# Attention and a mixture of experts in one kernel: three runs of score units a tile in place of four, and the values in one piece

## Chip, cores and metric

The kernel runs on one core of a Trainium2 chip. The metric is the device time of one execution in microseconds (us). The engines are named as in the profile: PE (TensorE), DVE (VectorE), ACT (ScalarE), POOL (GpSimd) and SP (SyncE, which here only issues DMAs).

## The reference

Multi-query attention (8 batches, 16 heads, 384 positions, head size 64, one key and value head a batch) is followed by a two-level mixture of experts over the 3072 tokens of 1024 features that come out of it:

```
scores = scale * q @ k.T                 # per batch and head, 384 x 384
attn   = softmax(scores)
x      = (attn @ v), heads side by side  # 3072 x 1024
g      = argmax(x @ w_group)             # one of 4 groups, with its softmax weight g_w
e      = argmax(x @ w_expert[g])         # one of 4 experts of the group, weight e_w
out    = g_w * e_w * (relu(x @ w1[g, e]) @ w2[g, e])
```

## The kernel before

The attention is worked in *tiles* of 128 query positions for all 16 heads: three tiles a batch, 24 in all (the number `t`). A tile has eight *units* of two heads each (`u`). For a unit, `scores` (L198) makes 128 x 2 x 384 scores in PSUM; `soft` (L212) takes their row maximum on DVE (L217) and their exponentials with row sums on ACT (L220), into a buffer `pr` in SBUF. `norm` (L229) takes the reciprocal of the sums on DVE and multiplies on POOL. `transp` (L239) transposes a unit in 32 x 32 blocks on DVE into `ring`, which holds three half tiles. When all eight units of a tile stand there, `pv` (L246) multiplies them with the values into four PSUM banks, and `pv_out` (L263) copies these to SBUF, and POOL casts them to bf16.

PSUM has eight banks. Before, `ps_s` holds two score buffers of two banks each, and `ps_x` four single banks that `xbank` (L93) hands out in turn for everything else: values, expert matmuls, logits, transposed queries, counts.

All instructions of an engine run in the order in which the program writes them (the scheduler is set to manual). The main loop (L794) goes over *slots*, each of two units, so four slots a tile (`p` is the slot in its tile). In slots 0 and 1 the PE, after the scores, works on the expert of the batch before: `main_expert` is a generator that `advance(n)` (L710) moves on by n groups. A group is one PSUM bank of eight matmuls and its evacuation: 8 groups of the first layer, w1 (L479, 384 columns, relu on ACT in L485), and 6 of the second, w2 (L493, 512 columns, scaled on ACT in L511, here called y groups). In slots 2 and 3 PE does the two halves of the values of the tile before. Other steps hang on a slot and a place in it by `at` and are called by `run`: `logits` and the gate's small operations (`gate_first` on DVE, `gate_choose` on PE, `gate_score` on DVE, ...), which pick the expert that most tokens of the batch need, and the loads of the next q, k, v and of the expert's weights (4 MB, issued by POOL).

Transposed queries come in two ways. For the first five tiles (`TQ = 5`) `q_group` (L174) transposes on PE and copies with ACT (L187); later ones come by a DMA that leaves only a block transpose to DVE, `q_blocks` (L190).

After the last slot, from L827, a tail finishes the last tile, then computes the last batch's main expert, a second expert for the few tokens of it that need one (`few_...`), and a loop for the remaining ones.

Of the kernel before, what the change touches and what calls it, by code (L numbers as in the profile page):

```python
# [19 lines left out]
def kernel(  # L20
# [70 lines left out]
    TQ = 5  # L91

    def xbank():  # L93
        x = ps_x.tile([P, 512], FP32, tag="x", name="x")
        return x

# [100 lines left out]

    def scores(u):  # L198
        b, j, c = units[u]
        qt, kt = st["qt", u // 8, c // 4], st["kt", b]  # L200
        s = ps_s.tile([P, 2, 512], FP32, tag="s")
        cc = c % 4
        for h in range(2):
            r = slice(h * D, (h + 1) * D)
            for m in range(2):
                nc.tensor.matmul(  # L206
                    out=s[m * D:(m + 1) * D, h, 0:S], lhsT=qt[r, ts(2 * cc + m, D)], rhs=kt[r, :],
                    start=True, stop=True, tile_position=(h * D, m * D),
                )
        st["s", u] = s  # L210

    def soft(us, between):  # L212
        ssum = ppool.tile([P, 2, 2], FP32, tag="ssum")
        for k, u in enumerate(us):
            s = st.pop(("s", u))
            nmx = ppool.tile([P, 2], FP32, tag="nmx")
            nc.vector.tensor_reduce(out=nmx[:], in_=s[:, :, 0:S], axis=AX.X, op=ALU.max, negate=True)  # L217
            pr = ppool.tile([P, 2, S], FP32, tag="pr")
            for h in range(2):
                nc.scalar.activation(  # L220
                    out=pr[:, h, :], in_=s[:, h, 0:S], func=ACTF.Exp, bias=nmx[:, h:h + 1], scale=1.0,
                    accum_out=ssum[:, k, h:h + 1],
                )
            st["pr", u] = pr
            if k == 0:
                between()
        st["ssum", us[0]] = ssum

    def norm(us):  # L229
        rinv = ppool.tile([P, 2, 2], FP32, tag="rinv")  # L230
        nc.vector.reciprocal(out=rinv[:], in_=st.pop(("ssum", us[0]))[:])  # L231
# [14 lines left out]
    def pv(t, n0, n1):  # L246
# [3 lines left out]
        if n0 == 0:  # L250
            st["o", t] = [xbank() for _ in range(P // 32)]
        o = st["o", t]
# [10 lines left out]
    def pv_out(t):  # L263
# [6 lines left out]
        for i, o in enumerate(st.pop(("o", t))):  # L270
            nc.scalar.copy(out=xt[:, :, ts(i, 32)], in_=o[:, 0:2 * P].rearrange("p (c q) -> p c q", c=KO))  # L271
        nc.gpsimd.tensor_copy(out=st["xb", b][:, :, ts(j, P)], in_=xt)  # L272
# [254 lines left out]

    def any_bank():
        return bank_end() if st.get("ended") else xbank()[:]

    def main_expert(b, on_act):
# [5 lines left out]

        yield from expert(st["xb", b], w1, w2, scaled(lambda: st["gsel", b][0], store), any_bank, on_act)

# [164 lines left out]

    NSL = NU // 2
    SB = ST * 4
    NT = B * ST
    pending = []

    def advance(groups):  # L710
        for _ in range(3 * groups):
# [19 lines left out]
    for b in range(B):  # L731
        s0 = SB * b
        for x, j0, j1 in ((s0 + 8, 0, 1), (s0 + 16, 1, ST)):
            at(x, "m2", logits, b, j0, j1)
            at(x + 1, "m0" if b and j0 == 0 else "v", logits_out, b, j0, j1)
        at(s0 + 9, "m0" if b else "v", gate_first, b)
        at(s0 + 9, "m3" if b else "m2", gate_choose, b)
        at(s0 + 9, "w", gate_score, b)
        at(s0 + 9, "w", gate_pick, b)
        at(s0 + (13 if b == B - 1 else 12), "w", gate_picked, b)  # L740
        if b == B - 1:
            at(s0 + 9, "w", load_main, b, 0)
            at(s0 + 10, "w", load_main, b, 1)
        else:
            at(s0 + 9, "g", load_main, b, 0)
            at(s0 + 9, "g", load_main, b, 1)
            at(s0 + 16, "g", keep_xb, b)
        at(s0 + 17, "v", gate_masks, b)
        x = s0 + 18
        at(x, "e", gate_values, b)  # L750
        at(s0 + (19 if b == B - 2 else 22), "w", gate_selected, b)
        if b == B - 1:
            at(s0 + 13, "w", gate_pick_second, b)
        if b + 1 < B:
            at(s0 + 2, "g", load_k, b + 1)
            at(s0 + 4, "g", load_v, b + 1)
            at(s0 + 7, "g", scale_k, b + 1)
            at(s0 + 8, "e", k_blocks, b + 1)
    for t in range(NT):
        for x, u, half in ((4 * t, t, 1), (4 * t + 1, t + 1, 0)):  # L760
            if u < TQ:
                at(x, "m1", q_group, u, half)
            elif u < NT:
                at(x, "e", q_blocks, u, half)
        if t < NT - 2:
            at(4 * t, "g", load_q, t + 2)

# [73 lines left out]
    pv(NT - 1, NB // 2, NB)  # L841
    pv_out(NT - 1)
    advance(1)
    load_second(1)
    advance(4)
    run(i + 4, "m2")
    pending.append(main_expert(b, lambda k: k < FO or k % 2 == 0))
    advance(1)
    run(i + 5, "v")
# [6 lines left out]
    advance(2)  # L856
    few_places()
    gate_count()
    advance(1)
    run(i + 6, "e")  # L860
    run(i + 10, "w")
    gate_remaining()
# [26 lines left out]
    )  # L889
    advance(3)  # L890
    few_gather()
    advance(2)
    ls_ps = xbank()
# [68 lines left out]
```

## Time and profile before

| | |
|---|---|
| median of 3 runs | 509.52 us (509.21 to 509.81) |
| the profiled execution, its own time | 508.39 us |
| its span, first to last instruction | 507.0 us |
| mean granted clock of PE | 0.997 of full speed |
| DMA traffic | 84.04 MB, mean 166 GB/s |

An engine's busy time can be read against the span, but PE's matmuls are pipelined and their ends are modelled, so the rows' starts are the safer numbers: the distance from one piece of PE work to the next is what the piece costs. A row of the timeline has its start, its length, engine, line, operation, output and inputs, and in square brackets the idle time of the engine before it and what ended that. In rows of matmuls an fp32 matmul counts twice, since it is issued as two passes.

### The profile page before, as it was taken

What the parts mean: (1) busy time and instruction counts of PE and PEld (TensorE: products, weight loads), DVE (VectorE), ACT (ScalarE), POOL (GpSimd) and SP (SyncE); (2) the same over time, 40 slices, a digit from 0 to 9 for tenths busy, and PEclk for the clock granted to TensorE, in tenths of its full rate; (3) what the DMA queues carried; (4) which work ended last, traced back from release to release, by engine and by line L of the source; (5) the groups of instructions that cost most, each with busy time, mean ns of one, the idle gap of its engine ahead of it and who ended that gap; (6) DMA issues with size and microseconds to landing.
All of it is one profiled execution on the core that took longest, in us unless ns stands there. A gap on an engine that the chain in (4) does not pass through costs nothing.

```text
span 507.0 us, 20054 instructions
## 1 busy us (share of the span) xinstructions
PE 481.5 (95%) x8256; PEld 262.1 (52%) x8273; DVE 413.0 (81%) x737; ACT 321.8 (63%) x1002; POOL 289.6 (57%) x524
## 2 busy tenths in 40 slices
PE   7597789999999999999999999999999999999994
PEld 3143356555456455555465455555455455555653
DVE  3889979988899879988899879998799888890630
ACT  4776766677676766676676776676775775753421
POOL 1665955684576664584576654584476654584300
PEclk9999999999999999999999999999999999999998
DMA  7612997399947998389946998389956993089993
GB/s 106 145 26 45 174 239 193 76 160 233 255 86 129 220 237 218 75 157 232 261 84 123 217 243 223 75 143 230 245 116 111 210 241 110 1 155 241 231 243 121
DMA packets 64524, 84.04 MB, mean 166 GB/s; under 512 B 20379, under 2 KB 39963, under 8 KB 64432
## 3 DMA queue, kind: packets, MB, share of 16 engines
q0 software_dynamic: 19152, 37.84, 41.3%
q1 hardware_dynamic: 44320, 44.61, 35.2%
q8 instruction: 66, 1.08, 0.9%
q10 hardware_dynamic: 960, 0.30, 0.3%
q14 instruction: 26, 0.21, 0.1%
HBM read 101.52 MB, written 19.40 MB: 239 GB/s over the span
## 4 chain that ended last, share of the span: by engine, by line
PE 90%; DVE 5%; ACT 3%; issue 1%; POOL 0%; POOLq 0%; ACTq 0%; DVEq 0%
PE x L257 26%; PE s L206 25%; PE x L479 15%; PE x L493 13%; PE sb L493 4%; PE x L280 3%; ACT pr L220 3%; DVE nmx L217 2%; PE sb L479 2%; DVE ring L241 2%; PE x L674 1%; PE x L100 1%; PE x L689 1%; PE x L145 0%; PE x L643 0%
## 5 line engine op out<-in xcount | busy, mean ns | idle before, releaser
L235 POOL TENSOR_SCALAR pr<-pr,rinv 128x384 f32<-128x384 f32 x384 | 218.3, 588 | 146.0 <-DVE rinv L231 133.2
L220 ACT ACTIVATE pr<-s,nmx 128x384 f32<-128x384 f32 x384 | 218.0, 579 | 131.5 <-DVE nmx L217 120.0
L217 DVE TENSOR_REDUCE nmx<-s 128x2 f32<-128x768 f32 x192 | 174.3, 948 | 45.7 <-PE s L206 44.6
L241 DVE STREAM_TRANSPOSE ring<-pr 128x768 f32<-128x768 f32 x192 | 175.4, 952 | 0.1
L206 PE MATMUL s<-kt,qt 64*64 64x384 f32 x1536 | 148.9, 496 | 13.3 <-ACT pr L220 12.3
L257 PE MATMUL x<-ring,v_sb 32*64 32x256 f32 x4608 | 137.7, 378 | 0.2
L257 PEld LDWEIGHTS x<-ring,v_sb 32*64 32x64 f32 x4608 | 101.6, 131 | 43.0 <-issue 23.2
L206 PEld LDWEIGHTS s<-kt,qt 64*64 64x64 f32 x1536 | 48.5, 132 | 82.6 <-ACT pr L220 44.4
L220 ACT ACTIVATION_READ_ACCUMULATOR pr<-s,nmx 128x1 f32 x384 | 77.9, 203 | 0.0
L479 PE MATMUL x<-xb,w 128*128 128x384 bf16 x448 | 76.6, 326 | 0.0
L479 PEld LDWEIGHTS <-w 128*128 128x128 bf16 x512 | 47.7, 98 | 42.2 <-issue 12.6
L493 PE MATMUL x<-w,h_t 128*128 128x512 bf16 x276 | 64.7, 380 | 0.6
L493 PEld LDWEIGHTS <-h_t 128*128 128x128 bf16 x384 | 35.7, 98 | 52.0 <-issue 11.9
L454 POOL DMA_DIRECT2D w<-in_moe_w_dram x36 | 27.9, 784 | 10.8 <-issue 9.0
L271 ACT COPY xt<-x 128x256 f32<-128x256 f32 x96 | 28.9, 385 | 2.8 <-PE x L257 2.7
L485 ACT ACTIVATE h_t<-x 128x384 bf16<-128x384 f32 x56 | 25.4, 502 | 6.4 <-PE x L479 6.4
L272 POOL CAST xb<-xt 128x1024 bf16<-128x1024 f32 x24 | 24.9, 1036 | 3.6 <-ACT xt L271 3.6
L511 ACT ACTIVATE y<-x,gsel 128x512 f32<-128x512 f32 x36 | 24.8, 693 | 3.1 <-PE x L493 3.1
L195 DVE STREAM_TRANSPOSE qt<-q_sb 128x512 f32<-128x512 f32 x38 | 26.1, 687 | 0.0
L493 PE MATMUL sb<-w,h_t 128*128 128x512 bf16 x92 | 21.2, 379 | 0.2
L231 DVE RECIPROCAL rinv<-ssum 128x4 f32<-128x4 f32 x96 | 13.9, 144 | 3.3 <-ACT pr L220 3.3
L511 ACT ACTIVATE y<-sb,gsel 128x512 f32<-128x512 f32 x9 | 6.2, 688 | 16.1 <-PE sb L493 16.1
(132 smaller groups left out, 165.6 us busy)
## 6 DMA issues: line engine op xcount, KB each, us to landing
w<-in_moe_w_dram POOLq DMA_DIRECT2D x36, 1024.0 KB, 19.6
q_sb<-in_q_dram SPq DMA_DIRECT2D x76, 224.0 KB, 6.0
out_dram<-y SPq DMA_DIRECT2D x96, 128.0 KB, 6.3
xb_scratch<-xb SPq DMA_DIRECT2D x8, 768.0 KB, 4.3
v_sb<-in_v_dram SPq DMA_DIRECT2D x32, 96.0 KB, 4.0
kk<-in_k_dram SPq DMA_DIRECT2D x28, 92.0 KB, 4.1
q_sb<-in_q_dram SPq DMA_DIRECT2D x16, 128.0 KB, 3.3
q_sb<-in_q_dram SPq DMA_DIRECT2D x5, 64.0 KB, 3.1
```

Of the source, the lines that this page charges most:

```text
L195: nc.vector.transpose(out=qt[:].rearrange("p (x d) -> p x d", d=32), in_=q_sb[:, :, 0:32])
L206: nc.tensor.matmul(out=s[m * D:(m + 1) * D, h, 0:S], lhsT=qt[r, ts(2 * cc + m, D)], rhs=kt[r, :], start=True, stop=True, tile_position=(h ...
L217: nc.vector.tensor_reduce(out=nmx[:], in_=s[:, :, 0:S], axis=AX.X, op=ALU.max, negate=True)
L220: nc.scalar.activation(out=pr[:, h, :], in_=s[:, h, 0:S], func=ACTF.Exp, bias=nmx[:, h:h + 1], scale=1.0, accum_out=ssum[:, k, h:h + 1],)
L235: nc.gpsimd.tensor_scalar(out=pr, in0=pr, scalar1=rinv[:, k, h:h + 1], scalar2=1.0, op0=ALU.mult, op1=ALU.mult)
L241: nc.vector.transpose(out=ring[:, (u // 4) % 3, u % 4].rearrange("p h s -> p (h s)"), in_=st.pop(("pr", u))[:].rearrange("p h s -> p (h s)"),)
L257: nc.tensor.matmul(out=o[i][h * D:(h + 1) * D, 0:2 * P].rearrange("d (g c q) -> d g c q", g=2, c=4), lhsT=v_sb[r, n, :], rhs=ring[r, a:z + ...
L271: nc.scalar.copy(out=xt[:, :, ts(i, 32)], in_=o[:, 0:2 * P].rearrange("p (c q) -> p c q", c=KO))
L454: nc.gpsimd.dma_start(out=w[:, o:o + 4, :], in_=(w1f, w2f)[n][ds(e, 1), :, o:o + 4, :].rearrange("o p c f -> (o p) c f"))
L479: nc.tensor.matmul(out=hp[:, 0:S], lhsT=w1[:, ko, ts(fc, P)], rhs=xb[:, ko, :], start=(ko == 0), stop=(ko == KO - 1))
L493: nc.tensor.matmul(out=yp, lhsT=h_t[:, fo, ts(j, P)], rhs=w2[:, fo, ts(nh, 512)], start=(fo == 0), stop=(fo == FO - 1),)
L511: nc.scalar.activation(out=y[:, ts(nh, 512)], in_=yp, func=ACTF.Copy, scale=g)
```

## The change

A tile's eight units now come in three slots, of three, two and three units, in place of four slots of two. The third unit of a slot takes its scores in a buffer `e` of two banks of its own (`ps_e`, through `pair`), and the same buffer serves as two of the four banks of `pv`; `ps_x` shrinks from four banks to two. In slots 0 and 2 of a tile PE works on the expert (six or nine thirds of a group, in three parts, since `advance` now counts thirds), in slot 1 on the values of the tile before, all 12 blocks in one piece. Of a tile's eight transposes three now lie in slot 0 (the last units of the tile before), two in slot 1 and three in slot 2. The fourth of the value copies in `pv_out` goes to DVE (in the tail the second too). The expert of a batch starts at slot 3 of the nine of the next batch, where it was slot 5 of twelve. All hooks move to the new slots; `q_group` of the next tile's first half now lies in the third slot of the tile before, and both `q_blocks` in the middle slot.

```
-    ps_x = ctx.enter_context(tc.psum_pool(name="ps_x", bufs=4))
+    ps_e = ctx.enter_context(tc.psum_pool(name="ps_e", bufs=1))
+    ps_x = ctx.enter_context(tc.psum_pool(name="ps_x", bufs=2))
...
+    def xtile():
+        x = ps_x.tile([P, 512], FP32, tag="x", name="x")
+        return x[:]
+
+    def pair():
+        e = ps_e.tile([P, 2, 512], FP32, tag="e", name="e")
+        return e
+
     def xbank():
-        x = ps_x.tile([P, 512], FP32, tag="x", name="x")
-        return x
+        if not st.get("ended"):
+            return xtile()
+        n = st["banks"] = st.get("banks", -1) + 1
+        if n % 4 == 2:
+            st["pair"] = pair()
+        return st["pair"][:, n % 4 - 2, :] if n % 4 > 1 else xtile()
...
-    def scores(u):
+    def scores(u, spare):
...
-        s = ps_s.tile([P, 2, 512], FP32, tag="s")
+        s = pair() if spare else ps_s.tile([P, 2, 512], FP32, tag="s", name="s")
...
     def soft(us, between):
...
-            if k == 0:
-                between()
+            between(k)
...
         if n0 == 0:
-            st["o", t] = [xbank() for _ in range(P // 32)]
+            e = pair()
+            st["o", t] = [e[:, 0, :], e[:, 1, :], xtile(), xtile()]
...
         for i, o in enumerate(st.pop(("o", t))):
-            nc.scalar.copy(out=xt[:, :, ts(i, 32)], in_=o[:, 0:2 * P].rearrange("p (c q) -> p c q", c=KO))
+            xo, o = xt[:, :, ts(i, 32)], o[:, 0:2 * P].rearrange("p (c q) -> p c q", c=KO)
+            if i == 3 or (st.get("ended") and i == 1):
+                nc.vector.tensor_copy(out=xo, in_=o)
+            else:
+                nc.scalar.copy(out=xo, in_=o)
...
-    NSL = NU // 2
-    SB = ST * 4
+    NSL = B * ST * 3
+    SB = ST * 3
...
+        x = s0 + 6
+        at(x, "v", gate_first, b)
+        at(x, "m2", gate_choose, b)
+        at(x, "w", gate_score, b)
+        at(x, "w", gate_pick, b)
...
     for t in range(NT):
-        for x, u, half in ((4 * t, t, 1), (4 * t + 1, t + 1, 0)):
-            if u < TQ:
-                at(x, "m1", q_group, u, half)
-            elif u < NT:
-                at(x, "e", q_blocks, u, half)
+        if t < TQ:
+            at(3 * t, "m1", q_group, t, 1)
+        if t + 1 < TQ:
+            at(3 * t + 2, "m1", q_group, t + 1, 0)
+        elif t + 1 < NT:
+            at(3 * t + 1, "e", q_blocks, t + 1, 0)
+            at(3 * t + 1, "e", q_blocks, t + 1, 1)
...
+    U0 = (0, 3, 5, 8)
     for i in range(NSL):
-        t, p = i // 4, i % 4
-        if i >= SB + 5 and (i - 5) % SB == 0:
-            pending.append(main_expert((i - 5) // SB - 1, lambda k: True))
-        us = (2 * i, 2 * i + 1)
-        for u in us:
-            scores(u)
+        t, p = i // 3, i % 3
+        if i >= SB + 3 and (i - 3) % SB == 0:
+            pending.append(main_expert((i - 3) // SB - 1, lambda k: True))
+        us = range(8 * t + U0[p], 8 * t + U0[p + 1])
+        ready = [u for u in (range(8 * t - 3, 8 * t), range(8 * t, 8 * t + 2), range(8 * t + 2, 8 * t + 5))[p] if u >= 0]
+        for n, u in enumerate(us):
+            scores(u, n == 2)
         run(i, "s")
-        soft(us, lambda: run(i, "b"))
-        if p < 2:
-            run(i, "m0")
-            advance(1)
-            run(i, "m1")
-            advance(1)
-            run(i, "m3")
-            if p == 1 and t % ST > 0:
-                advance(1)
-        elif t > 0:
-            pv(t - 1, (p - 2) * NB // 2, (p - 1) * NB // 2)
+        if p == 1:
+            soft(us, lambda k: None)
+            if t > 0:
+                pv(t - 1, 0, NB)
+        else:
+            soft(us, lambda k: advance(3) if k == 1 else None)
+            run(i, "m1")
+            advance(2)
+            if ready:
+                transp(ready.pop(0))
+            advance(1)
+            if i % SB in (3, 8):
+                advance(2)
+                if ready:
+                    transp(ready.pop(0))
+                advance(1)
         run(i, "v")
         run(i, "m2")
-        if i >= 2:
-            transp(2 * i - 4)
-            transp(2 * i - 3)
+        for u in ready:
+            transp(u)
         run(i, "w")
         norm(us)
         run(i, "e")
-        if p == 3 and t > 0:
+        if p == 1 and t > 0:
             pv_out(t - 1)
         run(i, "g")
...
     st["ended"] = True
-    transp(2 * i - 4)
-    transp(2 * i - 3)
-    advance(2)
-    transp(2 * i - 2)
-    transp(2 * i - 1)
-    run(i + 1, "w")
-    advance(1)
+    advance(6)
+    for u in range(NU - 3, NU):
+        transp(u)
+    run(i, "w")
     load_second(0)
     few_ready()
     pv(NT - 1, 0, NB // 2)
-    advance(1)
+    advance(3)
     pv(NT - 1, NB // 2, NB)
     pv_out(NT - 1)
-    advance(1)
+    advance(3)
     load_second(1)
```

More of the change, by code (lines that the diff above doesn't have):

```diff
@@ L212, in soft @@
     def soft(us, between):
-        ssum = ppool.tile([P, 2, 2], FP32, tag="ssum")
+        ssum = ppool.tile([P, len(us), 2], FP32, tag=f"ssum{len(us)}", name="ssum", bufs=3)
         for k, u in enumerate(us):
@@ L536, in store @@
                 nc.sync.dma_start(out=out_v[b, j, n], in_=y[32 * n:32 * (n + 1), :])
-        yield from expert(st["xb", b], w1, w2, scaled(lambda: st["gsel", b][0], store), any_bank, on_act)
+        yield from expert(st["xb", b], w1, w2, scaled(lambda: st["gsel", b][0], store), lambda: bank_end() if st.get("ended") else xbank(), on_act)
     def few_ready():
@@ L699, in few_expert, with advance @@
         )
[L705 to L706 removed]
+    NSL = B * ST * 3
+    SB = ST * 3
     NT = B * ST
     pending = []
[L710 to L711 removed]
+    def advance(thirds):
+        for _ in range(thirds):
             while pending:
@@ L732 @@
         s0 = SB * b
-        for x, j0, j1 in ((s0 + 8, 0, 1), (s0 + 16, 1, ST)):
+        last = b == B - 1
+        for x, j0, j1 in ((s0 + 5, 0, 1), (s0 + 11, 1, ST)):
             at(x, "m2", logits, b, j0, j1)
[L735 to L740, printed above, removed]
@@ new lines @@
+        at(s0 + 16, "w", gate_selected, b)
+        if not last:
+            at(s0 + 1, "g", load_k, b + 1)
+            at(s0 + 3, "g", load_v, b + 1)
+            at(s0 + 5, "g", scale_k, b + 1)
+            at(s0 + 7, "e", k_blocks, b + 1)
+    for t in range(NT):
+        if t < TQ:
[5 more added lines that the diff above has]
+            at(3 * t + 1, "e", q_blocks, t + 1, 1)
```

53 lines of the change are left out of this document (23 added, 30 removed).

## The prediction

> **What bounds the kernel now.** I read the page first: the busy line of the engines and the head line of the chain that ended last.
>
> ```profile
> PE 481.5 (95%) x8256; PEld 262.1 (52%) x8273; DVE 413.0 (81%) x737; ACT 321.8 (63%) x1002; POOL 289.6 (57%) x524
> PE 90%; DVE 5%; ACT 3%; issue 1%; POOL 0%; POOLq 0%; ACTq 0%; DVEq 0%
> ```
>
> TensorE carries the chain. A mean hides stages, so next the table by windows: a piece of the head, where no expert work exists yet, and one steady batch of three tiles.
>
> ```profile
> 8.70:23.50 14.80, 8.35 (x74) 2.50 (x72) 11.71 (x18) 11.16 (x37) 8.45 (x15) 1.00 0.69 120
> 190.60:247.80 57.20, 57.10 (x1011) 30.85 (x1011) 50.68 (x86) 38.98 (x123) 35.03 (x61) 1.00 0.84 180
> ```
>
> In the steady batch PE is busy 57.10 of 57.20 us: nothing is gained there by feeding PE sooner, only by giving it less to do. VectorE has 6.5 us to spare. In the head PE works 8.35 of 14.80 us, so a loop over the other engines sets the pace. What PE does in the steady part is in the chain by time (start, us, what):
>
> ```profile
> 247.82 4.01 PE x L479 x24
> 253.28 2.78 PE x L257 x96
> 265.25 1.45 PE s L206 x16
> 266.70 2.71 PE x L479 x16
> 285.65 3.56 PE x L493 x16
> 305.15 4.01 PE x L479 x24
> ```
>
> From 247.82 to 305.15, the same place one batch later, are 57.33 us, without holes. The pieces have a fixed part: w1 matmuls cost (4.01-2.71)/8 = 0.16 each, so 2.71 is 16 x 0.16 + 0.15. A 256-column fp32 pass at that rate (384 columns in 0.16) costs two times 0.107, with eight in the array at once: 96 of them are 12 x 0.213 = 2.56, and the values piece of 2.78 has 0.22 over. Now one slot, from the timeline; this gives every latency that I use.
>
> ```profile
> 252.14 0.15 PEld L206 LDWEIGHTS s<-kt,qt 64*64 64x64 f32 x4 [0.17 <-issue]
> 252.46 0.15 PEld L206 LDWEIGHTS s<-kt,qt 64*64 64x64 f32 x4 [0.17 <-issue]
> 252.82 1.78 DVE L217 TENSOR_REDUCE nmx<-s 128x2 f32<-128x768 f32 x2
> 253.83 0.58 ACT L220 ACTIVATE pr<-s,nmx 128x384 f32<-128x384 f32 x1 [1.33 <-DVE nmx L217]
> 254.53 1.81 DVE L241 STREAM_TRANSPOSE ring<-pr 128x768 f32<-128x768 f32 x2
> 254.96 0.58 ACT L220 ACTIVATE pr<-s,nmx 128x384 f32<-128x384 f32 x1
> 256.27 0.13 DVE L231 RECIPROCAL rinv<-ssum 128x4 f32<-128x4 f32 x1
> 256.50 2.27 POOL L235 TENSOR_SCALAR pr<-pr,rinv 128x384 f32<-128x384 f32 x4 [1.82 <-DVE es L416]
> ```
>
> Half a unit of scores every 0.32, so a unit is 0.64 and a piece of n units 0.17 + 0.64n (two: 1.45). A maximum takes DVE 0.855 (two from 252.82 to 254.53), a transpose 0.87 (two to 256.27), a unit's exponentials 1.13 on ScalarE (253.83 to 254.96), the reciprocal comes 1.31 after the last unit's first exponential, and Pool normalizes a unit in 1.14, beginning 0.23 after it. The head gives the links between engines:
>
> ```profile
> 6.76 1.52 PE L206 MATMUL s<-kt,qt 64*64 64x384 f32 x16 [0.24 <-ACT qt L187]
> 7.71 1.82 DVE L217 TENSOR_REDUCE nmx<-s 128x2 f32<-128x768 f32 x2 [1.51 <-PE s L206]
> 8.70 0.58 ACT L220 ACTIVATE pr<-s,nmx 128x384 f32<-128x384 f32 x1 [1.71 <-DVE nmx L217]
> 9.99 0.88 PE L206 MATMUL s<-kt,qt 64*64 64x384 f32 x8 [1.12 <-ACT pr L220]
> 14.39 0.59 ACT L187 COPY qt<-x 128x512 f32<-128x512 f32 x1
> ```
>
> Scores to maximum 0.95, maximum to exponential 0.99, exponential to a free score buffer 1.29 (1.13 and 0.16 for the signal), and a copy of transposed queries 0.59.
>
> **The change, part by part. (1) Fewer pieces on PE.** A tile goes from four score pieces and two value pieces to three and one: 0.17 + 0.22 = 0.39 us less, 1.17 a batch. Expert pieces stay two a tile. From tile 5 on 19 tiles remain, 6.33 batches: 7.4 us at most.
>
> **(2) New stalls in the steady part.** Rows for what stands near the values:
>
> ```profile
> 250.54 0.88 ACT L485 ACTIVATE h_t<-x 128x384 bf16<-128x384 f32 x2
> 260.34 1.20 ACT L271 COPY xt<-x 128x256 f32<-128x256 f32 x4
> 268.10 0.18 DVE L302 TENSOR_REDUCE mx<-lg 128x5 f32<-128x20 f32 x1
> 268.53 0.18 DVE L306 TENSOR_TENSOR first<-oh 128x16 bf16<-128x16 f32 x1
> 269.24 0.17 PE L341 MATMUL x<-first,ones 128*128 128x16 bf16 x1
> ```
>
> Call T the start of a tile's scores. In its first slot DVE does three maxima from T+0.95 and then three transposes, of the last units of the tile before, to 0.95 + 2.57 + 2.61 = 6.1; all values matmuls wait for them (about T+6.3). PE needs 2.09 for scores, 0.15 + 2.56 for two w1 groups and 1.45 for the next scores: 6.25. With two y groups (3.42) it is 7.1, with three w1 groups 7.5. So DVE just keeps up. The exception is the tile with gate_first: 0.6 us of small operations (268.10 to 268.71) go ahead of two of the transposes, and gate_choose, now on PE behind the groups, waits for them: 5.0 against 4.8, 0.2 lost; then transposes and gate_score end near 6.9 against 6.5, 0.2 more. With only two banks for expert groups the third group of a slot, and logits, wait for the ScalarE evacuation (0.44, row 250.54) behind two units' exponentials: 0.95 + 0.99 + 2.26 + 0.44 + 0.16 = 4.8 against PE's 4.8; I take 0.1 twice. Sum 0.6 a batch; net gain 1.17 - 0.6 = 0.57, over 6.33 batches **-3.6**. The third unit's wait for the two shared banks costs nothing: values end, two copies of 0.30 (1.20 for four) free them by about +1.0, while the other two units' scores hold PE for 1.45. Were ScalarE late, each 0.1 over that would be paid in every tile. The fourth copy moves to DVE: between 0.30 (ScalarE's) and 0.56 (a 384-column PSUM read in the row below); I take 0.35, nearer in size to the first, and it lies where DVE waits for the values anyway. Three reciprocals less a batch return 0.3, so DVE needs some 51.5 of 56.6 us: still not the bound. Pool, DMA issues and loads keep their distances in time.
>
> **(3) The head.** Here the move of query groups costs most. For the first five tiles q_group's copy stands on ScalarE behind all three units' exponentials, and the very next scores need it. A three-unit slot is then a loop: 0.95 + 0.99 + 3 x 1.13 + 0.59 + 0.16 = 6.1 before the next slot (or its second unit) can be scored. The middle slot is 0.8 for that unit and 5.34 for the values in one piece, with the following scores behind it and DVE idle. Tile: 6.1 + 0.8 + 5.34 + 6.1 = 18.3. Tile 0, without values, by the same links is 14.8. The start slips 0.4: with two banks the first query transposes wait for the evacuation of K's.
>
> ```profile
> 5.64 0.56 DVE L151 TENSOR_SCALAR kt<-x 128x384 f32<-128x384 f32 x1 [3.70 <-PE x L145]
> 5.92 0.60 PE L183 MATMUL x<-ident,q_sb 128*128 128x128 f32 x4
> 72.83 0.58 ACT L220 ACTIVATE pr<-s,nmx 128x384 f32<-128x384 f32 x1 [0.72 <-DVE nmx L217]
> 88.58 1.52 PE L206 MATMUL s<-kt,qt 64*64 64x384 f32 x16
> ```
>
> First exponential now 8.70, that of tile 4 at 72.83. After: 9.1 + 14.8 + 3 x 18.3 + 0.1 for the gate = 78.9, **+6.1**. Tile 4 now takes from 70.9 (72.83 less 1.94) to 88.58, 17.7, with three expert groups. After, it has five and a query group: 2.09 + 0.15 + 3 x 1.28 + 0.6 and about 1.2 of waits for two banks (the third group behind the query copy) = 7.9; 1.45 + 5.34; then 2.09 + 2.71 and logits 0.7: 20.2, **+2.5**. It has two groups more done for that.
>
> **(4) The tail**, timeline of PE after the last slot:
>
> ```profile
> 451.13 5.35 PE L493 MATMUL sb<-w,h_t 128*128 128x512 bf16 x23
> 456.41 2.85 PE L257 MATMUL x<-ring,v_sb 32*64 32x256 f32 x96
> 459.19 1.90 PE L493 MATMUL sb<-w,h_t 128*128 128x512 bf16 x7
> 461.02 3.61 PE L257 MATMUL x<-ring,v_sb 32*64 32x256 f32 x96
> 464.56 3.63 PE L493 MATMUL sb<-w,h_t 128*128 128x512 bf16 x15
> 468.12 1.10 PE L280 MATMUL x<-xt,wge 128*32 128x64 f32 x64
> 469.15 1.47 PE L479 MATMUL sb<-xb,w 128*128 128x384 bf16 x8
> ```
>
> Now 18.0 from 451.13 to 469.15, with six y groups. After, four: two groups (3.6), then the last three transposes are awaited until +4.15 (three units through Pool, 3.4), 2.78 values, 1.86, 2.78, 1.86, 1.03 logits: 14.5. Less 0.4 for the last slot, where the first y group waits for a late relu: **-3.1**. From 469.15 on nothing changes.
>
> **Sum**: +6.1 + 2.5 - 3.6 - 3.1 = +1.9 on the profiled execution's own 508.39: 510.3. That lies 1.13 under the median 509.52, so 511.4.
>
> [...] The row first: five matmuls of 512 columns on the cold array took 2.32 us, 0.46 each, where the y group above needs 3.56/16 = 0.22; in the head now PE never rests 3 us and the granted clock is 1.00.
>
> ```profile
> 1.67 2.32 PE L100 MATMUL x<-blank 128*128 128x512 bf16 x5 [1.67 <-DVE blank L74]
> ```
>
> After, PE rests in each third slot of the head from about 2.8 to 6.1. [...]
>
> **Rivals.** (A) The stalls of (2) don't come: then -7.4 in place of -3.6, and 511.4 - 3.8 = 507.6, **faster**. It decides if transposes are done before PE reaches the values, that is if DVE enters each tile no later than T+0.95. For it: DVE's 6.5 us spare a batch. Against: in the gate tile the order alone makes it late. (B) The one-piece values wait in every tile for DVE or for the second evacuation, 0.5 each: 19 x 0.5 = 9.5 in place of 3.8, 517.1. For it: three margins of 0.1 to 0.3 us in (2). (C) The clock drops in the head: at the start the array took from 1.67 to some time before 6.76 to come up to speed, so tiles 0 to 3 would each do some 4 us of PE work at half rate, +2 each, 519.4. [...] (D) The 0.39 is not saved, because the fixed parts belong to the neighbours: +7.4, 518.8; against it, the overhang appears in pieces of every kind.
>
> **How the numbers follow.** Forecast 0.52, by itself 509 to 514; A 0.24; B 0.14; C 0.05; D 0.05. Two in ten outside: 507 to 517.5, which takes in A and B. This kernel's measurement tells 0.2% (1.0 us) from no change: faster 0.27 (A and the forecast's edge), same 0.14, slower 0.59.
>
> **What would show it.** In the changed profile: a batch about 56.6 us, value pieces of 5.3, score pieces of 2.1 with three units; tile 4's first exponential near 79; first tiles of 18.3 in which scores wait for the query copy; the tail 3 us shorter. A steady batch of 56.0 means A, above 58 means B or D. A head under 74 us would make the forecast wrong on its largest term.

## The result, and the profile after

The changed kernel takes 547.4 us (median of 4 runs, 545.22 to 548.47) against 509.37 us of the kernel before on the same chip: ratio 1.0745, interval 1.0708 to 1.0782. It is slower, as forecast, but by 38 us where 2 were forecast, far outside the range. The profiled execution took 547.32 us, its span is 545.9, 38.9 over the 507.0 of before. Here and below, a ratio compares fast executions alone; one that lies over 1.5% above the fastest of its kernel counts as slow.

First the page: the engines' busy line, the queue that brings instructions, and the head of the chain.

```profile
PE 492.7 (90%) x8273; PEld 282.1 (52%) x8273; DVE 418.4 (77%) x738; ACT 311.9 (57%) x977; POOL 289.8 (53%) x524
q8 instruction: 66, 1.08, 0.8%
PE 75%; DVE 12%; ACT 5%; issue 5%; POOL 1%; POOLq 0%; ACTq 0%; DVEq 0%
```

PE has 75% of the chain where it had 90%; VectorE has 12%, and 5% is "issue", time in which the engine waited for nothing that the profile shows. The mean granted clock fell from 0.997 to 0.975. Keep the second row in mind: PE's 16,546 instructions (8273 matmul passes and as many weight loads), and 66 packets of 16.4 KB (1.08 MB/66). If those are PE's instructions, a packet holds about 250.

Next the windows that stood in the prediction, the piece of the head and the same batch (start:end, length, busy time and instructions of PE, weight loads, DVE, ACT and POOL, granted clock, DMA share, GB/s):

```profile
8.70:23.50 14.80, 8.42 (x72) 2.79 (x68) 11.29 (x17) 10.40 (x34) 6.39 (x12) 0.88 0.69 119
206.40:268.00 61.60, 57.81 (x1014) 33.07 (x1011) 51.19 (x86) 37.71 (x121) 35.12 (x62) 1.00 0.77 166
```

The batch takes 61.6 us, not the 57.2 of before nor the 56.6 forecast. PE's work in it is 57.81, so nearly four microseconds are idle, at full clock. What PE waited for (total us, times, longest):

```profile
PE s L220 <- ACT qt L201: 15.9, 8, 3.3
PE e L271 <- issue: 11.4, 7, 2.4
PE x L271 <- issue: 6.9, 4, 2.4
PE e L669 <- DVE xg L664: 0.8, 1, 0.8
PE e L602 <- DVE xtok L606: 0.8, 1, 0.8
PE e L689 <- DVE few_h L695: 0.6, 1, 0.6
```

The first row is the head's query copy, forecast. The next two were not: 18.3 us in the values matmuls (L271) behind no other engine. The last three lie in the tail. The chain by time shows the holes (start, us, what):

```profile
210.55 1.45 PE s L220 x16
212.00 0.38 PE e L271 x4
...
216.35 0.14 PE e L271 x4
216.49 2.40 issue
...
220.40 1.45 PE s L220 x16
...
232.75 0.45 PE e L271 x4
...
238.19 1.45 PE s L220 x16
...
252.25 0.38 PE e L271 x4
...
256.30 0.97 issue
...
259.23 1.45 PE s L220 x16
```

The values matmuls run without a pause from 212.00 for 4.5 us, stand still in the middle of the piece with all inputs there and all banks free, and go on. From values to scores it is 8.4 us (212.00 to 220.40) and 7.0 (252.25 to 259.23), where the undisturbed piece (232.75 to 238.19) takes 5.4. The windows from each start show what lies beside it, in the DMA share (last but one) and the rate:

```profile
212.00:216.40 4.40, 4.40 (x154) 4.03 (x153) 4.37 (x9) 2.36 (x8) 4.31 (x8) 1.00 1.00 210
232.70:238.20 5.50, 5.45 (x196) 5.04 (x200) 5.43 (x13) 2.36 (x8) 4.76 (x8) 1.00 0.02 6
252.20:256.30 4.10, 4.10 (x142) 3.16 (x138) 4.10 (x7) 2.36 (x8) 3.59 (x7) 1.00 1.11 254
```

The whole piece runs undisturbed where the DMA engines are idle. All pieces from tile 6 on, from the first matmul's start to the next piece's, each column the slots of one tile of a batch:

| kernel | first tile | second tile | third tile |
|---|---|---|---|
| changed | 7.35 7.11 6.97 7.45 6.77 8.15 | 8.97 8.39 8.13 7.85 7.96 5.58 | 5.37, six times |

5.37 is the forecast (5.34); 26.2 us of the 18 pieces lie over it. That is the greater part of the loss. Of it 18.3 us are the idle time on issue, in 11 holes; the rest lies in the same pieces, two of which run on at half clock for a while (from 156.45 and 443.17 us). The stretches divide at these rows of PE's timeline (88.58, 451.13 and 469.15 are those of before, in the prediction):

```profile
100.62 1.52 PE L220 MATMUL s<-kt,qt 64*64 64x384 f32 x16
...
490.41 3.62 PE L511 MATMUL sb<-w,h_t 128*128 128x512 bf16 x16
...
505.43 0.82 PE L497 MATMUL sb<-xb,w 128*128 128x384 bf16 x4
```


| stretch | before | after | forecast | measured |
|---|---|---|---|---|
| start to the scores of tile 5 | 88.58 | 100.62 | +8.6 | +12.0 |
| 19 tiles, to the tail's first y groups | 362.55 | 389.79 | -3.6 | +27.2 |
| from there to the logits' end | 18.02 | 15.02 | -3.1 | -3.0 |
| logits' end to the end | 37.85 | 40.47 | 0 | +2.6 |

### The profile page after: what moved, and what is told of

It is laid out like the page before. It is cut to its first block, busy times and chain, and to the rows that moved or that the text cites. A ratio compares the mean times of both kernels' runs of the same rounds, so it can differ in the third digit from the quotient of the medians.

```text
span 545.9 us, 20002 instructions
## 1 busy us (share of the span) xinstructions
PE 492.7 (90%) x8273; PEld 282.1 (52%) x8273; DVE 418.4 (77%) x738; ACT 311.9 (57%) x977; POOL 289.8 (53%) x524
## 2 busy tenths in 40 slices
DMA packets 64524, 84.04 MB, mean 154 GB/s; under 512 B 20379, under 2 KB 39963, under 8 KB 64432
## 3 DMA queue, kind: packets, MB, share of 16 engines
q8 instruction: 66, 1.08, 0.8%
## 4 chain that ended last, share of the span: by engine, by line
PE 75%; DVE 12%; ACT 5%; issue 5%; POOL 1%; POOLq 0%; ACTq 0%; DVEq 0%
PE e L271 18%; PE s L220 16%; PE x L511 12%; PE x L497 10%; PE x L271 7%; DVE nmx L231 5%; DVE ring L254 5%; ACT pr L234 4%; PE e L220 4%; PE sb L511 3%; PE x L298 2%; PE sb L497 2%; POOL pr L248 1%; ACT qt L201 1%; PE x L114 1%
## 5 line engine op out<-in xcount | busy, mean ns | idle before, releaser
L234 ACT ACTIVATE pr<-s,nmx 128x384 f32<-128x384 f32 x288 | 163.5, 579 | 108.0 <-DVE nmx L231 92.7
L231 DVE TENSOR_REDUCE nmx<-s 128x2 f32<-128x768 f32 x144 | 131.0, 948 | 30.6 <-PE s L220 29.8
L271 PE MATMUL e<-ring,v_sb 32*64 32x256 f32 x2304 | 135.9, 379 | 13.5 <-issue 11.4
L271 PE MATMUL x<-ring,v_sb 32*64 32x256 f32 x2304 | 136.4, 380 | 6.9 <-issue 6.9
L220 PE MATMUL s<-kt,qt 64*64 64x384 f32 x1152 | 118.4, 526 | 17.1 <-ACT qt L201 15.9
L271 PEld LDWEIGHTS e<-ring,v_sb 32*64 32x64 f32 x2304 | 92.5, 132 | 36.5 <-issue 20.8
L271 PEld LDWEIGHTS x<-ring,v_sb 32*64 32x64 f32 x2304 | 98.0, 132 | 11.9 <-issue 11.2
L289 ACT COPY xt<-e 128x256 f32<-128x256 f32 x47 | 15.2, 375 | 76.4 <-PE x L271 55.5
L234 ACT ACTIVATION_READ_ACCUMULATOR pr<-s,nmx 128x1 f32 x288 | 58.3, 202 | 0.0
L234 ACT ACTIVATE pr<-e,nmx 128x384 f32<-128x384 f32 x96 | 55.7, 601 | 0.0
L231 DVE TENSOR_REDUCE nmx<-e 128x2 f32<-128x768 f32 x48 | 45.5, 948 | 0.3 <-PE e L220 0.3
L220 PE MATMUL e<-kt,qt 64*64 64x384 f32 x384 | 40.6, 493 | 0.0
## 6 DMA issues: line engine op xcount, KB each, us to landing
w<-in_moe_w_dram POOLq DMA_DIRECT2D x36, 1024.0 KB, 17.1
```

Source lines behind the costliest of these rows:

```text
L220: nc.tensor.matmul(out=s[m * D:(m + 1) * D, h, 0:S], lhsT=qt[r, ts(2 * cc + m, D)], rhs=kt[r, :], start=True, stop=True, tile_position=(h ...
L234: nc.scalar.activation(out=pr[:, h, :], in_=s[:, h, 0:S], func=ACTF.Exp, bias=nmx[:, h:h + 1], scale=1.0, accum_out=ssum[:, k, h:h + 1],)
L271: nc.tensor.matmul(out=o[i][h * D:(h + 1) * D, 0:2 * P].rearrange("d (g c q) -> d g c q", g=2, c=4), lhsT=v_sb[r, n, :], rhs=ring[r, a:z + ...
L289: nc.scalar.copy(out=xo, in_=o)
```

## The experiments

Two theories for the holes. **Supply**: PE's instructions are brought in blocks by DMA (the instruction packets above). Values in one piece are the densest long stretch of the program, 192 passes with their weight loads, so 384 instructions in 5.37 us; where a block's border falls early in it and other transfers delay the fetch, PE has used up what it holds before the next block is there. **Banks**: a value bank, shared with the third unit, or some wait that the profile doesn't resolve, comes free late.

The trace of the changed kernel itself bears on this, since it keeps the start and the length of each of the 66 packets. Each of the 11 holes ends 1.2 to 1.5 us after one of these packets has ended. And from one hole to the next are 768 and 1280 instructions in turn, to within one (those of PE's sequencer counted in), three and five times 256: all 11 holes lie at borders of 256 instructions. Around the hole from 216.49 to 218.89, in the window 212 to 222, there is one instruction packet among 2189 others:

```profile
q1 hardware_dynamic: 2189, 1.93, 95.9%
q8 instruction: 1, 0.02, 0.9%
```

It starts at 216.13 and takes 1.41 us. PE had crossed the border before, 256 instructions earlier, at 212.55, so the packet began 3.6 us after that. From tile 6 on to the last, a packet begins 0.3 to 1.0 us after such a border where the DMA engines are idle, and 2.2 to 4.5 us after it where their share is 0.9 to 1.1; its own length goes from 0.88 to no more than 1.44. The values use up 256 instructions in 3.45 us. So the packets beside traffic start late, rather than take long. The experiments ask what a hole needs.

**Values in halves again**, in the changed kernel's middle slot of tiles 1 and on:

```
+            if not (p == 2 and t > 0 and n < 2):
                 scores(u, n == 2)
...
-                pv(t - 1, 0, NB)
+                pv(t - 1, 0, NB // 2)
+                for u in (8 * t + 5, 8 * t + 6):
+                    scores(u, False)
+                pv(t - 1, NB // 2, NB)
```

> The changed kernel, with the values of slot 1 cut into two halves again and the scores of the next slot's first two units put between them; all else as changed. Theory S (supply): the holes of 1.0 to 2.8 us inside 15 of the 24 values pieces are PE running out of instructions, because one piece uses up instructions faster (384 weight loads and matmuls in 5.4 us) than their next block comes; then between the halves the supply catches up, the holes go (under 3 us left of 27), and the time falls from 547 to 517 to 523. Rival B (banks): values and third unit wait for each other over the two shared banks, whatever the length of the piece; then the holes stay and the time stays within 540 to 548.

561.55 us, ratio 1.1012 (1.0988 to 1.1036): slower still. The waits:

```profile
PE e L220 <- ACT xt L289: 15.4, 23, 0.7
PE e L271 <- issue: 6.7, 7, 1.4
PE x L271 <- issue: 1.4, 2, 1.0
```

The idle time on issue halves, but with the two units' scores taken away from behind the values, nothing covers the two copies that free the shared banks: 0.7 us in every tile. The prediction had named that cover (1.45 us of scores against +1.0). The run can't tell the theories apart by its time, and the 8.1 us on issue that are left are more than the 3 that the supply theory allowed.

**One piece in the kernel before**, which has four banks and shares none: values of both halves in slot 2, none in slot 3.

```
-        elif t > 0:
-            pv(t - 1, (p - 2) * NB // 2, (p - 1) * NB // 2)
+        elif t > 0 and p == 2:
+            pv(t - 1, 0, NB)
```

> The kernel before, with the values as one piece in slot 2 of a tile and none in slot 3, with its four banks of their own; no third units, no shared banks. Theory S: holes of 1 to 3 us marked as issue appear inside values pieces, in many of the tiles from the sixth on, 10 to 30 us in sum. Rival B: none appear, since nothing is shared. The total time also grows by 2 us or so a tile for another reason (slot 3 has no filler for PE), so it is the holes that are read, not the total.

583.63 us. Two losses stand in its waits:

```profile
PE s L206 <- ACT pr L220: 55.1, 62, 1.8
PE x L257 <- issue: 9.6, 7, 2.0
```

The first is of this kernel's own making (slot 3 has no PE work behind the scores). The second is what was asked: holes on issue in values that share nothing, with pieces of 8.28, 7.98, 9.56, 9.06 and 8.21 us in one tile of five successive batches. The shared banks aren't needed for them. Each of the seven ends 1.3 to 1.5 us after an instruction packet. They are fewer than expected, 9.6 us where 10 to 30 were named.

**Without the expert weights' loads** of batches 1 to 7 (the first batch's weights are used throughout; 54.67 MB moved instead of 84.04, no PE instruction changed):

> The changed kernel, with the expert weights of batches 1 to 7 not loaded (those of batch 0 are used again: 28 of the 84 MB of DMA are left out). Theory S with a late refill under DMA traffic (S+D): the holes in each batch's first tile (values pieces of 6.8 to 8.2 us, which lie over the weight loads) go, some 12 us in sum, and those of each second tile (7.9 to 9.0 us, which lie over loads of q and v and stores) stay: 533 to 537. Theory S without any part of the DMA: all holes stay, 546 to 548. A theory of traffic alone would take away the first ones too, but can't explain why the kernel before, with the same traffic, has none.

```profile
PE x L271 <- issue: 7.5, 3, 2.6
PE e L271 <- issue: 4.9, 2, 2.7
```

Of six first-tile pieces five fall to 5.37 and one to 5.78; of the second-tile pieces five stay at 8.8 to 9.5. The place is as expected, the time is not: 544.0 us, 3.4 less, for the second tile's pieces grew by 4 us in all, and the clock fell to half behind each of its five holes (2.3 to 2.7 us): six half-speed stretches of 3.41 us in the steady part, where the changed kernel has two.

**Without the q loads** of tiles 7 to 23:

```
+        if t >= TQ + 2:
+            st["q", t] = st["q", t - 2]
+            return
```

> The changed kernel with the q loads of tiles 7 to 23 left out: those tiles compute on an older tile's q (17 loads of about 0.8 MB each are left out; every instruction of TensorE stays). If TensorE runs out of fetched instructions because the block that it needs comes late behind other transfers, the values pieces of each batch's second tile, which lie in the burst of the q loads, fall from 7.9-9.0 us towards 5.4, while those of the first tile, which lie beside the weight loads, keep their 6.8-8.2; the idle time put down to issue ahead of L271 falls from 18 us to 8-12, and the time to 527-538. If the transfers have no part in it, both tiles keep their long pieces and the time stays at 545-548.

```profile
PE e L274 <- issue: 5.4, 4, 1.6
PE x L274 <- issue: 2.4, 2, 1.4
```

The mirror image: second-tile pieces are 5.58 in all six, first-tile pieces stay (7.12, 7.11, 6.92, 7.40, 7.35, 7.58). 531.75 us, 15.6 less. So it takes the traffic: each load makes the holes beside which it lies, and those alone.

**Moved borders**: 64 small matmuls, 128 instructions, in the changed kernel's first tile and nothing else.

```
+            if i == 2:
+                x = xbank()
+                for _ in range(64):
+                    nc.tensor.matmul(out=x[:, 0:64], lhsT=blank[:, 0:P], rhs=blank[:, 0:64], start=True, stop=True)
```

> The changed kernel, with 64 matmuls of 64 columns on zeros (128 instructions of PE) added in a stretch of the head where PE rests; nothing else. Theory S: instructions come in blocks of 256 (66 packets of 16 KB on the instruction queue); a hole comes only where a block's border lies in the first quarter of a values piece, so that the whole next block is used up inside the piece. Moving all borders by half a block takes most holes away: 20 to 27 us less, 521 to 530 (and the head's clock may stay up, 2 us more). Rival: holes follow from the piece and the traffic alone, and a shift by 128 instructions changes nothing: 546 to 549.

534.94 us: with more work, 12.5 us less. Of the pieces from tile 6 on one is long (7.02), the other 17 take 5.37 to 5.65. The holes that are left lie elsewhere:

```profile
PE s L220 <- issue: 3.4, 3, 1.7
PE e L220 <- issue: 1.3, 3, 0.5
```

So it takes the place in the program too. The time missed the expected range by 5 us: the head's slow stretches stayed, with a values piece of 7.97 among them.

**The same in the kernel before**: 103 small matmuls, 206 instructions, in its first tile.

> The kernel before with 103 small matmuls (206 instructions) added in the first tile, about 10 us of them at most and in idle time in part. If the holes come from the place of the borders of 256 instructions in the program, and the kernel before is free of them only because its borders fall elsewhere, moving all later borders puts idle time on issue of 8 to 12 us in all into its values halves or scores, and the time is 516-526. If halved values are safe wherever the borders lie, idle time on issue stays below 3 us and the time is 509-514.

509.98 us, against 508.67 of before beside it: the rival was right, and my expectation wrong.

```profile
PE x L257 <- issue: 1.2, 2, 0.9
PE x L280 <- issue: 1.0, 1, 1.0
```

Halved values, with 1.45 us of sparse scores between them, hold out at this place of the borders as well. What made holes in these runs isn't the place alone: it took the dense piece, a border early in it, and traffic.

**Query copies ahead of the third unit's exponentials**, in the changed kernel:

```
-            soft(us, lambda k: advance(3) if k == 1 else None)
-            run(i, "m1")
+            soft(us, lambda k: (run(i, "m1"), advance(3)) if k == 1 else None)
```

> The changed kernel with the copies of the transposed queries put ahead of the third unit's exponentials. If the third unit's three matmul groups wait in the head for the query copy queued behind those exponentials (15.9 us in 8 waits), that wait falls below 10 us and the head shortens by 5 to 9 us: 538-542, with the holes in the steady tiles as they were. If VectorE's copies bound the head, the wait moves to them, and the gain is at most 2 us: 545-548.

```profile
PE s L220 <- ACT qt L201: 7.9, 8, 2.1
PE e L271 <- issue: 14.5, 8, 2.8
PE x L271 <- issue: 7.8, 4, 2.5
```

The wait is halved and the third values piece starts at 63.47 instead of 69.14, 5.7 us sooner. But that piece now has a hole too (10.06 us), and in all the holes cost 4 us more: 546.86. The cause in the head was right; the gain was eaten, and the time fell into the range that the expectation had kept for another cause.

**Borders that keep their place.** Counted over the trace, a batch of the changed kernel has 2039 PE instructions, those of its sequencer among them: 8 x 256 less 9. And the hole begins 258, 267, 276, 285, 294 and 303 instructions into the first tile's values of successive batches, and 299, 308, 317, 326, 335 into the second tile's: 9 further each time. That is what a border every 256 instructions does. So: query copies early, 72 instructions in the first tile, and ten more a batch to end the drift.

```
-        nc.tensor.matmul(
-            out=c_ps[:, 0:GE], lhsT=ones[:], rhs=st.pop(("first", b))[:].rearrange("p g e -> p (g e)"),
-            start=True, stop=True,
-        )
+        first = st.pop(("first", b))[:].rearrange("p g e -> p (g e)")
+        for _ in range(6):
+            nc.tensor.matmul(out=c_ps[:, 0:GE], lhsT=ones[:], rhs=first, start=True, stop=True)
```

> The changed kernel with the query copies early, 72 more TensorE instructions in the first tile and 10 more per batch (a small matmul of the gate repeated five times, same sum), so that the instruction count of a batch comes to 8 blocks of 256 and the borders keep their place. If the holes are a matter of where the borders fall, under 5 us of idle time on issue is left, nearly all values pieces take 5.4 us, and the time is 512-520: the kernel before is not beaten, since the head still costs some 5 us more. If the holes come from the one-piece values themselves, they stay and the time is 538-545.

530.48 us, ratio 1.043 (1.0387 to 1.0473). All 18 pieces now take 5.37 to 5.60. Yet the time is 10 us over the expected range; the chain of one batch says where:

```profile
187.75 1.44 PE s L220 x14
189.20 0.98 issue
```

The first tile's border lies later in the values, and the supply runs out just behind them, in the scores: 3.88 us in place of 2.10, once in every batch. The hole had moved, not gone.

**The border 42 instructions later** (15 small matmuls in place of 36):

> As the run with aligned borders (530.5 us), with 15 instead of 36 of the small matmuls in the first tile: 42 instructions fewer ahead of everything, so that the border that lay 173 instructions into the values of each batch's first tile, whose supply then ran out in the scores behind them (a piece of 3.88 us in place of 2.10, once a batch), lies 215 in, where the expert matmuls behind the scores use instructions slowly. By the theory of the borders that hole goes: 7 x 1.8 = 12 us less, 516-520. If borders are not what makes it, or if it only moves, 526-532.

523.46 us, ratio 1.0239 (1.0194 to 1.0283). The score piece behind the first tile's values is back at 2.10 us. But the second tile's border, 40 instructions away from the first's, has now come to the start of its values, and four pieces there take 6.7 to 7.5 us. Seven of the expected 12 us came; one shift can't suit both tiles.

**The pair's halves used one by one in the tail:**

```
-        if n % 4 == 2:
+        if n == 2:
             st["pair"] = pair()
```

> As the run before it, with the two banks of the pair handed out one by one in the tail (the pair is allocated once and its halves are used again by themselves, instead of a new pair for every second bank). If the 2.65 us that the tail lost after the logits are the waits for both halves of a pair, this run takes 2 to 3 us less than the one before it, and the three waits of 0.6 to 0.8 us for xtok, xg and few_h fall away. If not, the two agree within 1 us.

521.11 us, ratio 1.0221 (1.0199 to 1.0242), but the waits for xg, xtok and few_h stand unchanged (0.8, 0.8, 0.6) and the stretch behind the logits takes 40.5 us in both runs; the 2.3 us between the medians lie elsewhere. This edit failed to test what it was meant to test.

**Pauses filled**: 18 matmuls of 128 columns behind the query transposes in two slots of each of tiles 0 to 3, in place of the 15 small ones.

```
+            if t < 4:
+                x = xbank()
+                for _ in range(18):
+                    nc.tensor.matmul(out=x[:, 0:P], lhsT=blank[:, 0:P], rhs=blank[:, 0:P], start=True, stop=True)
```

> As the run before it, with the small matmuls of the first tile replaced by 18 of 128 columns behind the query transposes in each of 8 slots of tiles 0 to 3 (the same number of instructions modulo 256). They shorten TensorE's longest pauses in the head by about a microsecond. If the halved clock there follows pauses of 2.6 us and more, the granted clock stays at full speed in the head and the run takes 2 to 5 us less than the one before it: 509-513. If the clock drops for another reason, the drops stay, and the time is the same or 1 to 3 us longer.

The windows of the head, first of the run before it, then of this one:

```profile
5.80:70.00 64.20, 49.09 (x822) 27.32 (x829) 51.00 (x77) 38.96 (x128) 35.10 (x60) 0.87 0.56 101
```

```profile
5.80:70.00 64.20, 54.40 (x1053) 35.85 (x1056) 52.72 (x81) 40.83 (x134) 38.74 (x66) 0.97 0.58 109
```

The clock rises from 0.87 to 0.97, and the sixth values piece starts at 120.79 us instead of 124.68 (118.84 before the change). The median is 522.87, though, ratio 1.028 (1.0232 to 1.0327), between 519.76 and 527.02, while the run above lay between 519.98 and 524.2, and 509 to 513 was expected. Executions of this one kernel differ by 7.3 us, more than the 3.9 us that the head gained, so the medians can't show the gain. That the steady tiles' holes make the difference is likely, not shown: the two runs above have the same program up to the tail, and their second-tile pieces took 6.71 7.19 7.54 6.71 5.58 5.58 in the one trace and 6.87 5.58 6.99 5.58 6.71 6.17 in the other. The profiled execution took 519.76.

**Three banks in turn in the tail**, the pair used as one, and 16 instructions more in the head:

```
-        if n == 2:
-            st["pair"] = pair()
-        return st["pair"][:, n % 4 - 2, :] if n % 4 > 1 else xtile()
+        return pair()[:, 0, :] if n % 3 == 2 else xtile()
```

> As the run with the pauses filled, with two edits that show in different stretches. In the tail the pair is used as one bank (its first half), so that three banks take turns and no matmul writes one half while the other is read. If the three waits of 0.8, 0.8 and 0.6 us were there because the halves count as one buffer, they fall away or below 0.3 us and the stretch behind the logits takes about 2 us less (38.5 in place of 40.5); if four turns were needed, other waits of the same size come. And 19 in place of 18 small matmuls a slot put the borders 16 instructions further: the second tile's border lies 12 instructions ahead of where it was, so that by the theory of the borders its fetch goes out ahead of the burst more often, and fewer than four of the seven second tiles show a values piece over 6 us. Both right: 513-519; neither: 520-525.

The PE timeline of the second expert, first of the changed kernel, then of this one:

```profile
532.91 1.06 PE L689 MATMUL e<-xg,w 128*128 128x128 bf16 x16
534.56 1.05 PE L689 MATMUL e<-xg,w 128*128 128x128 bf16 x16 [0.59 <-DVE few_h L695]
```

```profile
513.25 1.06 PE L686 MATMUL e<-xg,w 128*128 128x128 bf16 x16
514.14 1.06 PE L686 MATMUL x<-xg,w 128*128 128x128 bf16 x16
```

The second half of the pair had waited for the read of the first; now all three waits are gone, and the stretch behind the logits takes 38.7 us in place of 40.5 (37.85 before the change). The other half of the expectation failed: five second-tile pieces are over 6 us, one of them 10.05, in the profiled execution, which was one of the two long ones (527.1 us; five lay between 518.61 and 527.46). The holes came 17 instructions sooner by count than in the run above (227 for 244, 226 for 243), for the 16 that were added. With 256 to a block, the border before them lay 12 instructions ahead of the values in the run above and 29 ahead here; that is no safer than one behind their start. 522.56 us, ratio 1.0198 (1.016 to 1.0236).

No version beats the kernel before. The best trace (span 518.3) is 11.3 us over it: 2.0 to the sixth values piece, 7.5 from there to the last, where the pieces from tile 6 on lie 6.1 over 5.37, and 1.9 after.

## Why the prediction was wrong

**The step that failed is the steady part of the sum**, -3.6 by stalls of 0.6 a batch against a saving of 1.17; it measured +27.2. I had priced everything that PE waits for and taken its own supply of instructions as free. Issue was in the rows that I quoted, 1% of the chain before, and no piece of values before has more than 192 instructions between sparser ones. It was shown by the packets, behind which every hole ends, by taking away either traffic (first-tile holes go without the weights, second-tile holes without q), by moving the borders with work added (12.5 us less), and by holes in one-piece values without shared banks. Beside traffic the packet starts late, 2.2 to 4.5 us behind the border in place of 0.3 to 1.0. What holds its start back was not shown.

The rest of the steady part was right in kind. With the holes away, the values take 5.37 in the gate's tile and in the first (5.58 in the second; what the 0.2 is stays open), the score pieces 2.10, the scores wait for no bank. But the saving was put too large: in the best trace a batch without long pieces (218.86 to 275.95) takes 57.1 us (0.2 of it for the added gate matmuls) against 57.2 to 57.3 of before. Its scores cost 17.1 instead of 17.4, its values 16.3 instead of 16.65, and the w1 groups 11.06 instead of 10.71, of which 0.2 is the wait for the gate's `first`: the one takes half of the other back. So the forecast of 56.6 would have missed without holes too, by 0.3 us or more a batch.

Two further dips of the clock lie in the steady part, at 156.45 and 443.17. Each follows a hole, of 2.42 and 1.78 us, so these two cost clock besides their own time.

**The head** was +12.0, not +8.6. The loop was right: tile 1 takes 18.42 us (22.35 to 40.77 by its scores) against 18.3, and tile 4 20.1 against 20.2, and the query copy holds the scores as said, 15.9 us in 8 waits. What came on top is rival C, in part: tiles 2 and 3 take 20.72 and 19.03, with three-unit score pieces of 3.57 and 3.46 us for 2.10, at half clock. In tile 2 PE also waits 1.9 us for `first`, where 0.1 stood in the sum for the gate. Tile 4's first exponential came at 82.52 instead of 78.9. I had given C 0.05; that the pauses which I had estimated (from about 2.8 to 6.1) would leave the clock full was shown by no run. The windows show what went ahead of the half-speed stretches (the granted clock is the third figure from the end):

```profile
36.99:40.40 3.41, 1.22 (x68) 0.94 (x68) 3.41 (x5) 3.41 (x13) 0.00 (x0) 1.00 0.00 0
40.40:43.81 3.41, 3.04 (x20) 1.29 (x24) 1.85 (x5) 0.68 (x2) 2.65 (x5) 0.50 0.00 0
77.95:81.36 3.41, 1.61 (x55) 1.11 (x59) 2.99 (x6) 2.52 (x9) 0.45 (x1) 1.00 1.12 234
81.36:84.77 3.41, 3.17 (x32) 1.58 (x23) 3.31 (x4) 2.25 (x9) 2.95 (x6) 1.00 0.91 326
153.04:156.45 3.41, 0.99 (x34) 0.86 (x37) 0.54 (x1) 0.00 (x0) 2.32 (x7) 1.00 0.72 156
156.45:159.86 3.41, 3.41 (x43) 1.45 (x28) 1.05 (x2) 0.92 (x3) 1.04 (x1) 0.50 0.81 148
```

In the traces of the kernel before and the changed one, the granted clock changes only at whole steps of 3.41 us. Each of the seven half-speed stretches in the head and the steady part is one step long and follows one at full clock in which PE was busy 0.8 to 1.6 us of 3.41 (1.22 and 0.99 here); after 1.61 (the third row) it stayed full. In these two traces, up to 500 us, six steps at full clock had less than 1.6 us of PE's work, and half speed followed on each; on the 269 with more than 1.8 us full speed followed without exception; of the four between (1.61 to 1.75) half speed followed on one. The pause before the scores at 40.77 was 2.56 us, the longest pause in each of the seven 1.8 to 3.3. So the clock went with the work in a whole step, and pauses of 1.8 to 3.3 us were enough. The fill of the pauses agrees with it: a granted clock of 0.97 in the head in place of 0.87, and full after 20.5 us.

**The tail** up to the logits' end gave 3.0 us, forecast 3.1. "From 469.15 on nothing changes" was wrong by 2.6: a pair handed out as two banks is still one buffer, and 1.8 of it was shown to be that. The 0.8 left is open; three banks instead of four may be all.

**The rivals.** A's stalls came in the gate's tile: values began 6.9 us into it, as forecast, with waits of 0.4 a batch where 0.6 was forecast for all stalls. B's wait for banks didn't come, and D's fixed parts were saved in scores and values. None held the cause, and the sign "above 58 means B or D" pointed at two that weren't there. The 38.9 us are +12.0, +27.2, -3.0 and +2.6, and 26.2 of them lie in the values pieces. The direction would have come right without the holes too: head and tail alone make +11.6, more than the 7.4 that the steady part could have saved at most.

## What to carry to other kernels

In this kernel, with 192 small passes in one piece, the supply of instructions was a resource like a bank or a queue: count instructions per microsecond (256 in 3.45 us here), and look in the changed profile for idle time on "issue" in the middle of a piece whose inputs are all there. The sparse work between dense pieces wasn't only filling here: with 1.45 us of scores between halved values the kernel before had no hole in them, without it the same kernel had seven, of 9.6 us. A rearrangement that removes such work needs a trace of its own before any fixed part saved is counted as gain. Here a late packet took up to 4.5 us to begin, 1.4 to come and 1.5 to take effect; by this estimate from one trace, 256 instructions beside such traffic should last some 7 us. A buffer of two banks handed out as two single ones kept the waits of one here, three of 0.6 to 0.8 us.

## What the runs showed of the hardware

A border every 256 PE instructions: from hole to hole in the changed kernel are 768 or 1280, and the holes drift by 9 instructions a batch where a batch has 2039, and by -1 with ten more. The page's instruction packets rose from 66 to 67 with 128 instructions more and to 68 with 368 and 384 more. A values piece of 384 instructions, 5.37 us where nothing holds it, stood still on issue for 0.8 to 2.4 us beside weight or q loads, and never from tile 6 on in the third tile of the changed kernel's batches, which lies beside neither. From tile 6 to the last, an instruction packet of that kernel began 0.3 to 1.0 us behind the border where the DMA engines were idle, 2.2 to 4.5 us behind it where their share was 0.9 to 1.1, and PE went on 1.2 to 1.5 us after it had ended. In the traces of before and after the granted clock changed only at whole steps of 3.41 us; up to 500 us, half speed followed on each of the six steps at full clock with under 1.6 us of PE's work, and full speed on each of the 269 with over 1.8. Holes of 1.8 and 2.4 us in the changed kernel, and of 2.3 to 2.7 without the weight loads, went ahead of half clock.
